# Two banks of a layer-1 attention unit computed on VectorE from thirds of score tiles, and zeros written by transfers

## The chip, the core and the metric

The kernel runs on one core of a Trainium2 chip. The core has five engines with instruction streams of their own: TensorE (PE, with its weight loads PEld) for matmuls, VectorE (DVE), ScalarE (ACT, which computes exponentials), GpSimd (POOL) and SyncE (SP, which here only issues transfers). The metric is the device time of one execution, in microseconds; lower is better. Times of several runs are given with their median.

## The reference

Four attention layers stand one after the other over 2048 positions of width 640, with 32 heads of 20 values. Layers 0 and 2 look back over a window of 256 positions, layers 1 and 3 see all positions. Each adds its output to its input.

```python
def _B_ref(x, wqkv, wo):                      # _A_ref is the same with a mask: 0 <= q - k < 256
    qkv = (x @ wqkv).reshape(B, S, 3, H, Dh).transpose(2, 0, 3, 1, 4)
    q, k, v = qkv[0], qkv[1], qkv[2]
    scores = jnp.einsum("bhqd,bhkd->bhqk", q, k) * (Dh ** -0.5)
    p = _softmax(scores, axis=-1)
    o = jnp.einsum("bhqk,bhkd->bhqd", p, v)
    return o.transpose(0, 2, 1, 3).reshape(B, S, D) @ wo

x = A_x
x = x + _A_ref(_layernorm(x), A_wqkv, A_wo)   # layer 0
x = x + _B_ref(_layernorm(x), B_wqkv, B_wo)   # layer 1
x = x + _A_ref(_layernorm(x), A_wqkv, A_wo)   # layer 2
x = x + _B_ref(_layernorm(x), B_wqkv, B_wo)   # layer 3
```

## The kernel before

The work is cut into units. A unit is a layer, a chunk of 512 queries (c from 0 to 3) and a group of four heads (g from 0 to 7). For each block of 128 keys and each head it has one bank: a matmul of 128 keys by 512 queries that fills one of the eight banks of PSUM. A full unit (layers 1 and 3) has 16 key blocks times four heads, 64 banks; a unit with a window has 12. Layer 1's chunk 0 and layer 3's chunk 0 are done in parts, over ranges of keys (PARTS), since the later keys come into being only while the layer below is finished; their partial sums are kept in a large fp32 tile, part_o["t"] (named raw_o in the profile).

The main loop (the `while` near the end) makes one score tile per turn, a tick. In a tick PE writes the scores of the next three banks (L1186) into PSUM banks 0 to 2 or 3 to 5, in turn; ACT takes the exponential of the whole tile in one instruction (L1206) and writes it to SBUF as the tile pt; and PE multiplies the probabilities of four banks that are two or three ticks old by the values (L1258, "PV"), adding up in PSUM bank 7, called op. When a unit ends, DVE copies op to SBUF (oT, L805), and a tail of small steps on PE and DVE divides by the sums of the rows (L962 to L998). Units with a window have a mask multiplied in on DVE (L1241). Bank 6 serves everything else; it is given out by take_m and drop_m.

Between score tiles a planner places tasks: normalizing (t_ln), projections to q and k (t_block, evacuated by L304 and sent to DRAM from POOL at L507), values (t_v), the output projection (t_out), and tails. Each has a due time, the unit that first needs it, and a cost in PE time; pump() spends a credit per tick on them. The function keep_clock counts PE's activity over the last three ticks and puts in filler matmuls (L612) into bank 6 where there is too little. Weights, and q, k and v of a unit, are fetched by SP (load_unit, L711 to L733), the next unit's ahead of time (load_ahead).

In layer 3's chunks 1 to 3 (but for the first unit) the last key block of each head, four banks of 64, is set aside (Unit.aside). Its scores are written into bank 6 when that is free (L837), and DVE computes the exponential by arithmetic on the bits of the float: t_side yields one DVE instruction after another (L843 to L881, two heads at a time), and side_step takes as many as side["credit"] allows, which grows by SIDE_RATE each tick. side_start takes four tiles of the normalized input, which are free by then, as its work space. At the unit's end PE multiplies the results by the values (L1267).

The strips of 32 partitions that hold a head of 20 values need zeros in their last 12. At the start DVE sets slot 8 of the tile ka_all to zero (L154; PE's warm-up matmuls at L1036 read it too), and a task, t_zeros, lets DVE write zeros to slots 9 to 17 (L1009), the output weights wop (L1013), and the k and q tiles kts and qts (L1018), spread over ticks; then "kas" and "kts" are set as ready, which load_unit's callers ask for (unit_needs). After wop is zeroed, load_wop fetches the output weights into it through SP.

## Time and profile before

| | us |
|---|---|
| median of 5 runs | 2401.8 |
| the five runs | 2407.64, 2408.22, 2400.97, 2401.8, 2400.6 |
| the profiled execution | 2407.64 |
| its span, first to last instruction | 2405.9 |

The profile below is of that one execution. A group's line gives the source line, the engine, what is written and read with its shape, how often, the busy time and the mean duration; after the bar stands the engine's idle time just before these instructions and what ended it. Durations of instructions that follow each other closely overlap, so their sum can exceed the busy time that an engine could spend. A fresh start on one engine often waits for another; the views of waits say for whom. "Granted clock" is the share of its full rate at which TensorE ran.

### The profile page before, as it was taken

The page shows a single profiled execution, that of the slowest core. Times are in us where ns is not written, and L with a number is a line of the kernel's source. Part 1 is how long each engine was busy: PE and PEld are TensorE (multiplying, and loading weights), DVE is VectorE, ACT ScalarE, POOL GpSimd, SP SyncE. Part 2 cuts the span into 40 slices and gives each one's busy share as a digit, 9 for nine tenths or more (in the row PEclk, how much of TensorE's full clock was granted, in tenths as well). Part 3 has the DMA queues.
Part 4 walks back from the last instruction along what each step waited for, and adds up shares of the span by engine and source line. Part 5 has one row for each costly group of instructions (what it writes and reads, how often), then busy time and mean ns, then how long its engine had stood idle before and what let it go on. Part 6 is the DMA issues. An engine that isn't in the chain of part 4 may idle for free.

```text
span 2405.9 us, 40056 instructions
## 1 busy us (share of the span) xinstructions
PE 2024.0 (84%) x15761; PEld 729.1 (30%) x15761; DVE 1273.0 (53%) x2473; ACT 2199.5 (91%) x1738; POOL 136.2 (6%) x284
## 2 busy tenths in 40 slices
PE   7898898888888898888888888888788788888886
PEld 3343333323323342333322333332322121122112
DVE  6676776423323243423352434452667767777776
ACT  6787889899999999999999989999999989999995
POOL 2111110000000001000100001001000000000000
PEclk9798999998999999999998989999855565556556
DMA  3332422322200223102330124022200010111000
GB/s 110 85 94 68 110 69 59 76 62 68 81 19 26 57 71 90 34 13 56 88 91 16 19 74 112 26 41 74 63 29 26 26 37 26 30 34 37 26 13 11
DMA packets 172796, 129.11 MB, mean 54 GB/s; under 512 B 115584, under 2 KB 155904, under 8 KB 172608
## 3 DMA queue, kind: packets, MB, share of 16 engines
q1 hardware_dynamic: 163872, 101.39, 17.0%
q0 software_dynamic: 8736, 25.18, 3.0%
q8 instruction: 123, 2.02, 0.3%
q14 instruction: 65, 0.53, 0.1%
HBM read 98.70 MB, written 27.79 MB: 53 GB/s over the span
## 4 chain that ended last, share of the span: by engine, by line
ACT 37%; PE 31%; issue 16%; DVE 13%; DMA 2%; SPq 1%; POOL 0%; ACTq 0%; DVEq 0%; POOLq 0%
ACT pt L1206 34%; PE ps L1186 8%; PE ps L353 6%; PE ps L1258 5%; PE ps L529 4%; PE ps L612 3%; PE ps L444 3%; ACT ka L1206 2%; DVE pt L1241 2%; DVE st L304 1%; DMA wqk<-in_B_wqkv_dram 1%; DVE on L995 1%; DVE oT L805 1%; DVE xnT L864 1%; DVE x_sb L538 1%
## 5 line engine op out<-in xcount | busy, mean ns | idle before, releaser
L1206 ACT ACTIVATE pt<-ps 128x1536 bf16<-128x1536 f32 (+3 forms) x1586 | 2053.2, 1442 | 144.3 <-PE ps L1186 131.5
L1186 PE MATMUL ps<-qt,kt 32*128 32x512 bf16 x4004 | 641.4, 462 | 231.4 <-ACT pt L1206 174.7
L1258 PE MATMUL ps<-pt,vt 128*21 128x512 bf16 x3744 | 463.6, 453 | 17.6 <-DVE oT L805 15.9
L1186 PEld LDWEIGHTS <-kt 32*128 32x128 bf16 x4004 | 188.6, 94 | 631.6 <-issue 610.7
L1241 DVE TENSOR_TENSOR pt<-pt,masks 128x1024 bf16<-128x1024 bf16 (+5 forms) x403 | 240.8, 625 | 163.8 <-ACT pt L1206 162.7
L353 PE MATMUL ps<-xnT,wqk 128*128 128x512 bf16 x830 | 229.2, 403 | 19.7 <-DMA wqk<-in_B_wqkv_dram 5.5
L612 PE MATMUL ps<-masks,ident 128*128 128x512 bf16 x765 | 230.5, 412 | 7.2 <-DVE st L304 2.7
L1258 PEld LDWEIGHTS <-vt 128*21 128x21 bf16 x4004 | 103.6, 90 | 352.0 <-issue 341.0
L304 DVE CAST st<-ps 128x512 bf16<-128x512 f32 x127 | 87.8, 691 | 196.1 <-PE ps L353 195.3
L529 PE MATMUL ps<-wop,on 128*128 128x320 bf16 x968 | 174.5, 322 | 6.4 <-DVE x_sb L538 3.4
L1186 PE MATMUL ps<-qa,ka 32*128 32x384 bf16 (+2 forms) x1408 | 117.6, 280 | 32.8 <-ACT pt L1206 29.1
L995 DVE TENSOR_TENSOR on<-oT,ps 128x512 bf16<-128x512 bf16 x128 | 87.5, 684 | 107.0 <-PE ps L991 104.2
L538 DVE TENSOR_TENSOR x_sb<-x_sb,ps 128x320 bf16<-128x320 bf16 x120 | 58.1, 484 | 149.5 <-PE ps L529 149.5
L843 DVE TENSOR_SCALAR xnT<-ps 128x512 int32<-128x512 f32 x92 | 63.6, 691 | 128.2 <-PE ps L837 125.1
L1206 ACT ACTIVATE ka<-ps 128x2048 bf16<-128x2048 f32 x65 | 127.1, 1955 | 2.6 <-PE ps L1186 2.2
L444 PE MATMUL ps<-wv,xnT 128*128 128x320 bf16 x640 | 112.4, 309 | 5.7 <-DVE on L995 1.4
L529 PEld LDWEIGHTS <-on 128*128 128x128 bf16 x968 | 90.5, 103 | 76.7 <-issue 41.0
L353 PEld LDWEIGHTS <-wqk 128*128 128x128 bf16 x830 | 72.5, 100 | 121.3 <-issue 55.7
L805 DVE CAST oT<-ps 128x512 bf16<-128x512 f32 x112 | 76.8, 685 | 52.7 <-PE ps L1258 39.0
L612 PEld LDWEIGHTS <-ident 128*128 128x128 bf16 x765 | 67.6, 102 | 112.7 <-issue 74.8
L1258 PE MATMUL ps<-pt,va 128*21 128x384 bf16 (+2 forms) x1408 | 79.6, 292 | 16.8 <-DVE oT L805 12.7
L984 DVE COPY rT<-ps 32x128 bf16<-32x128 bf16 x128 | 26.7, 209 | 92.4 <-PE ps L982 91.9
(91 smaller groups left out, 1438.0 us busy)
## 6 DMA issues: line engine op xcount, KB each, us to landing
vt<-v_d SPq DMA_DIRECT2D x48, 336.0 KB
kt<-k_d SPq DMA_DIRECT2D x192, 80.0 KB
wqk<-in_B_wqkv_dram SPq DMA_DIRECT2D x80, 160.0 KB
wqk<-in_A_wqkv_dram SPq DMA_DIRECT2D x70, 160.0 KB
k_d<-st POOLq DMA_DIRECT2D x75, 128.0 KB, 2.2
q_d<-st POOLq DMA_DIRECT2D x75, 128.0 KB, 2.1
qt<-q_d SPq DMA_DIRECT2D x384, 20.0 KB
v_d<-vs POOLq DMA_DIRECT2D x16, 336.0 KB, 3.1
```

The costliest lines, as they stand in the source:

```text
L304: nc.vector.tensor_copy(out=out_, in_=in_)
L353: nc.tensor.matmul(pq, lhsT=wt[:, dc, :], rhs=xt[:, dc, :], start=(dc == 0), stop=(dc == KD - 1),)
L444: nc.tensor.matmul(pv, lhsT=xt[:, dc, i * P : (i + 1) * P], rhs=wv_sb[l % 2][:, dc, h * HD : (h + 1) * HD], start=(dc == 0), stop=(dc == K ...
L529: nc.tensor.matmul(yp, lhsT=on[:, g, qb * P : (qb + 1) * P], rhs=wop[:, g, i * HD : (i + 1) * HD], start=(last or g == 0), stop=(g == G - 1),)
L538: nc.vector.tensor_tensor(out=xv, in0=had, in1=yp, op=ALU.add)
L612: nc.tensor.matmul(ps[:, b, :], lhsT=ident[:], rhs=masks[:, 0, :], start=True, stop=True)
L805: nc.vector.tensor_copy(out=oT[:], in_=op)
L995: nc.vector.tensor_tensor(out=on[:, g, :], in0=oT[:], in1=zb, op=ALU.mult)
L1186: nc.tensor.matmul(sp[:, i, col * P : (col + qn) * P], lhsT=u.k(kc, j), rhs=u.q(j, q0, qn), start=True, stop=True,)
L1206: nc.scalar.activation(out=pt[:, i:k, b0 * P :], in_=sp[:, i:k, b0 * P :], func=ACT.Exp, scale=SCALE,)
L1241: nc.vector.tensor_tensor(out=pt_[:, i:k, b0 * P :], in0=pt_[:, i:k, b0 * P :], in1=mv_, op=ALU.mult,)
L1258: nc.tensor.matmul(op[32 * j : 32 * j + VW, q0 * P : (q0 + qn) * P], lhsT=u.v(kc, j), rhs=pt[:, i, col * P : (col + qn) * P], start=(first ...
```

## The change

It has two parts. First, slots 8 to 17 of ka_all are set to zero by one instruction at the start, and the zeros of wop, kts and qts are copied from them by transfers that POOL issues; t_zeros starts at its fifth tick instead of its thirteenth and has 11 transfers, one or two a tick, in place of 12 DVE memsets. "kas" is no longer asked for.

Second, in layer 1's chunks 1 to 3 two heads (2 and 3) have their last key block set aside: two banks of a unit's 64. Their scores are not written to bank 6 but as the third bank of a score tile whose other two banks go to ACT: when a tile of the unit is put together, the first time at its start and again three tiles later, two ordinary banks are taken and one that is set aside is added (`extra`). In that tick DVE reads the third bank (side["psum"]) into its work space, and ACT's exponential covers two banks, 1024 columns. The work space is part_o["t"], free between chunk 0's parts of layer 1 and those of layer 3 (side_early). The rest of t_side is the same code with a credit of 0.65 a tick. The last key block's ordinary group has then two banks for PV, and the results that DVE made are multiplied in at the unit's end, as in layer 3. Layer 3 sets aside what it did before, now written as `aside = (0, 1, 2, 3)`.

```diff
-    nc.vector.memset(ka_all[:, G : G + 1, :], 0.0)
+    nc.vector.memset(ka_all[:, G:KA, :], 0.0)
...
-                self.aside = l == 3 and c > 0 and (c, g) != (1, 0)
+
+                if c > 0 and (l, c, g) != (3, 1, 0):
+                    self.aside = (2, 3) if l == 1 else (0, 1, 2, 3)
                 k0, k1 = key_blocks(l, part)
-                kcs = range(k0, k1 - self.aside)
-                sets = [(None, 0, [(kc, 0, 4, 0)], j) for kc in kcs for j in range(4)]
+                sets = [
+                    (None, 0, [(kc, 0, 4, 0)], j) for kc in range(k0, k1) for j in range(4)
+                    if kc < NT - 1 or j not in self.aside
+                ]
...
-            return ["kas"] + [(n, l, c, b) for b in blocks for n in "qk"]
+            return [(n, l, c, b) for b in blocks for n in "qk"]
...
+    def side_early():
+
+        b = part_o["t"]
+        side["tiles"] = [b[:, 2 * n : 2 * n + 2, :].rearrange("p a b -> p (a b)") for n in range(3)]
+        side["tiles"].append(b[:, 6, :].bitcast(BF16))
+        side["out"] = deque([b[:, 7, :].bitcast(BF16).rearrange("p (a b) -> p a b", a=2)])
         side["gen"] = t_side()
+        side_step(False)
...
-                    mseq[0] += 1
-                    mfree[6] = (state["tick"] + 2, mseq[0])
-                    nc.tensor.matmul(
-                        ps[:, 6, :], lhsT=u.k(NT - 1, 2 * pair + i), rhs=u.q(2 * pair + i, 0, 4),
-                        start=True, stop=True,
-                    )
+                    xi, xm, xw, xe = side["tiles"]
+                    if u.l == 3:
+                        mseq[0] += 1
+                        mfree[6] = (state["tick"] + 2, mseq[0])
+                        nc.tensor.matmul(
+                            ps[:, 6, :], lhsT=u.k(NT - 1, u.aside[2 * pair + i]),
+                            rhs=u.q(u.aside[2 * pair + i], 0, 4), start=True, stop=True,
+                        )
+                        side["psum"] = ps[:, 6, :]
...
-                        out=xi.bitcast(I32)[:, i * C : (i + 1) * C], in0=ps[:, 6, :],
+                        out=xi.bitcast(I32)[:, i * C : (i + 1) * C], in0=side["psum"],
...
     def t_zeros():
-        yield ("wait", 12)
-        nc.vector.memset(ka_all[:, G + 1 : KA, :], 0.0)
-        ready.add("kas")
-        yield ("wait", 3)
+        z = ka_all[:, G : G + 4, :].rearrange("p a b -> p (a b)")
+        yield ("wait", 4)
         for n in range(2):
-            nc.vector.memset(wop[:, 4 * n : 4 * n + 4, :], 0.0)
-            yield ("wait", 3)
+            nc.gpsimd.dma_start(
+                out=wop[:, 4 * n : 4 * n + 3, :].rearrange("p g f -> p (g f)"), in_=z[:, 0 : 3 * D]
+            )
+            nc.gpsimd.dma_start(out=wop[:, 4 * n + 3, :], in_=z[:, 0:D])
+            yield ("wait", 1)
         load_wop(0)
         for t in (*kts, *qts):
-            for n in range(0, t.shape[1], S // 2):
-                nc.vector.memset(t[:, n : min(n + S // 2, t.shape[1])], 0.0)
-                yield ("wait", 3)
+            nc.gpsimd.dma_start(out=t[:], in_=z[:, 0 : t.shape[1]])
+            yield ("wait", 1)
         ready.add("kts")
...
+            u = banks[n][0]
+            at = placed.setdefault(id(u), [])
+            extra = []
+            if u.aside and len(at) < 2 and banks[n + 1][0] is u and len(tiles) >= 3 * len(at) + (at or [0])[0]:
+
+                extra = [(u, u.aside[len(at)], "side", 0, [(NT - 1, 0, 4, 0)], False, False, False)]
+                at.append(len(tiles))
+                size = 2
...
-            tiles.append(banks[n : n + size])
+            tiles.append(banks[n : n + size] + extra)
...
+                if cur[-1][2] == "side":
+                    cur = cur[:-1]
+                    n_b -= 1
+                    if side["gen"] is None:
+                        side_early()
+                    while side["at"] != "bank":
+                        side["credit"] = 0.1
+                        assert side_step(False)
+                    side["credit"] = max(side["credit"], 0.1)
+                    side["psum"] = sp[:, n_b, :]
+                    side_step(True)
...
-                side["credit"] = min(side["credit"] + SIDE_RATE, 1.2)
+                side["credit"] = min(side["credit"] + (SIDE_RATE if side["late"] else 0.65), 1.2)
...
-            if len(pts) >= 4 and pts[3][0] <= t - (3 if pts[0][3][0].windowed else 2):
-                group = [pts.popleft() for _ in range(4)]
+            u = pts[0][3][0] if pts else None
+            size = 4
+            if u is not None and u.aside and pts[0][3][4][0][0] == NT - 1:
+                size -= len(u.aside)
+            if len(pts) >= size and pts[size - 1][0] <= t - (3 if u.windowed else 2):
+                group = [pts.popleft() for _ in range(size)]
...
-                    for j in range(4):
+                    for n, j in enumerate(u.aside):
                         nc.tensor.matmul(
                             op[32 * j : 32 * j + VW, :], lhsT=u.v(NT - 1, j),
-                            rhs=pair[j // 2][:, j % 2, :], start=False, stop=True,
+                            rhs=pair[n // 2][:, n % 2, :], start=False, stop=True,
                         )
```

## The prediction

> **What bounds the kernel now.** I read the page's totals, then windows over stages, the groups by shape, the waits, the chain of waits and stretches of the timeline. The totals name the engine that is nearly always at work:
>
> ```profile
> PE 2024.0 (84%) x15761; PEld 729.1 (30%) x15761; DVE 1273.0 (53%) x2473; ACT 2199.5 (91%) x1738; POOL 136.2 (6%) x284
> ```
>
> ACT's exponentials fill 91% of the span, but stages differ. The windows over three stretches (columns: window and its length, busy time and count of PE, PE weight loads, DVE, ACT, POOL; then granted clock, DMA share, GB/s):
>
> ```profile
> 37.00:64.00 27.00, 17.46 (x146) 7.26 (x145) 25.26 (x64) 17.46 (x28) 1.47 (x2) 0.84 0.08 19
> ...
> 483.00:1391.00 908.00, 767.75 (x6316) 293.17 (x6315) 327.43 (x746) 864.05 (x660) 44.59 (x90) 0.94 0.21 53
> ...
> 1710.00:2370.00 660.00, 539.00 (x3407) 144.94 (x3407) 483.56 (x704) 635.08 (x449) 0.00 (x0) 0.55 0.10 28
> ```
>
> From 37 to 64 us, where the zeros are written, DVE is busy 25.26 of 27 us: DVE sets the pace. From 483 to 1391, nearly the whole of layer 1's chunks 1 to 3 (the last sum of chunk 0's parts starts at 501.1, the first partial sum of layer 3 is copied at 1440.6), ACT is busy 95% and DVE 36%. From 1710 to 2370, where layer 3 already has banks on DVE, DVE is busy 73% and ACT 96%. The third window is my yardstick for a DVE under such load. The waits of 483 to 1391 (total us, times, longest) say how ACT loses its other 5%:
>
> ```profile
> PE ps L1186 <- ACT pt L1206: 97.8, 212, 1.0
> ...
> ACT pt L1206 <- PE ps L1186: 39.2, 53, 2.1
> ```
>
> PE waits for ACT 97.8 us; ACT waits for PE 39.2 us (43 with all else). Those 39.2 us lie where PE is slow:
>
> ```profile
> 1028.22 2.32 PE L612 MATMUL ps<-masks,ident 128*128 128x512 bf16 x5
> ...
> 1031.65 18.91 ACT L1206 ACTIVATE pt<-ps 128x1536 bf16<-128x1536 f32 x14 [1.24 <-PE ps L1186]
> ...
> 1033.48 1.25 PE L612 MATMUL ps<-masks,ident 128*128 128x512 bf16 x5
> ```
>
> In the timeline five filler matmuls take 2.32 us at 1028, and 1.25 us at 1033; ACT starved 1.24 us at the slow ones. The middle line also gives ACT's pace when nothing starves it: 14 tiles in 18.91 us, 1.35 us a tile.
>
> **What the Trainium skill says.** (1) ScalarE: Activation LUTs, section "What ACT_TABLE_LOAD costs", gives an ACTIVATE with immediate scale 186 ns + 0.833 ns a column, with about 93 ns of overlap back to back. The trace agrees: 1.35 us between starts against 1.37 by that rule; and 2048-column tiles follow at 1.78 us (1819.17 to 1820.93 and the like), so a bank of 512 costs 0.43 us. (2) VectorE: DVE Perf Modes, section "The perf-mode tier table": tensor_tensor on fp32 stays at 1x, tensor_scalar on fp32 in SBUF gets 2x. The rows agree: 1221 ns against 694 ns for 1024 columns. (3) TensorE: Matmul & The Clock Gate, section "What's actually happening": the array runs at half rate after an idle window of about 3.4 us. The two filler rows above are that factor of nearly two. (4) SBUF — State Buffer, section "SBUF: two separate sides": DVE and GpSimd share a port pair that is held for a whole instruction, so DMAs issued from POOL can wait for DVE. No view here shows POOL blocked.
>
> **Part A, the zeros.** Removed: 12 DVE memsets. The chain of waits (start, length) holds four of them:
>
> ```profile
> 48.74 1.98 DVE ka L1009
> ...
> 55.66 1.12 DVE wop L1013
> ...
> 61.88 1.12 DVE wop L1013
> ...
> 99.57 0.48 DVE kt L1018
> ```
>
> The first three, 4.22 us, lie in the stretch where DVE is 94% busy. Without them DVE still has 21.0 us of work against 17.5 on PE and on ACT, so DVE stays the pace and all 4.2 us go. The kt memset adds 0.48. The other eight (70 to 130 us) lie beside PE and ACT: nothing. So -4.7.
>
> Added: the first memset grows from 256 to 2560 words. By the rows (272 ns for 256, 1978 ns for 2304: 0.833 ns a word) it takes 2.19 us, from 0.93 to 3.12. DVE's next work waits for a load until 4.39: hidden. PE's first warm-up matmul (reads this tile) starts at 2.75 now, so 0.4 us later, with the transposes behind the warm-up. +0.4; below that 0, as the later transposes wait for ACT anyway; above it +2 if the longer memset holds up POOL's mask work.
>
> Added: 11 transfers issued by POOL, four for wop, three kt, four qt, with the row of k_d's issue (551 ns): 6 us between about 25 and 37 us. POOL's L321 memsets of weight tiles stand among them, and DVE's L323 copies wait for those; POOL idles 1.2 to 2.0 us before each memset there, and at most two issues stand between two memsets. +0.4; bounds 0 and +3 (six memsets, 0.5 us each). On SP the four wop loads, with the wait for their zeros, now stand ahead of four wqk loads that were issued at 34.06; their first matmul is at 64.75, so some 30 us hide it: 0. The k and q loads into the zeroed strips come after 74: 0. The windowed loads no longer ask for "kas", but they wait for q and k of their chunk later than that: 0. **A = -4.7 + 0.4 + 0.4 = -3.9.**
>
> **Part B, two banks of each unit.** 24 units (chunks 1 to 3, eight each) give two banks to DVE: 48 score tiles have ACT take 1024 columns where it took 1536. The tile count stays, since the third bank rides in the tile.
>
> ```profile
> L1206 ACT ACTIVATE pt<-ps 128x1536 bf16<-128x1536 f32 x1360 | 1872.8, 1529 | 121.9 <-PE ps L1186 111.7 <-issue 6.2 <-ACT pt L1206 0.9
> ...
> L1206 ACT ACTIVATE pt<-ps 128x1024 bf16<-128x1024 f32 x145 | 149.6, 1033 | 18.8 <-PE ps L1186 16.8 <-DVE st L304 0.4 <-ACT pt L1206 0.2
> ...
> L843 DVE TENSOR_SCALAR xnT<-ps 128x512 int32<-128x512 f32 x92 | 63.6, 691 | 128.2 <-PE ps L837 125.1 <-ACT pt L1206 2.8
> ...
> L864 DVE TENSOR_TENSOR xnT<-xnT 128x1024 f32<-128x1024 f32 x46 | 56.2, 1221 | 0.7
> ...
> L848 DVE TENSOR_SCALAR xnT<-xnT 128x1024 int32<-128x1024 int32 x46 | 31.9, 694 | 1.6
> ```
>
> The means differ by 496 ns, but means contain overlap; I take the pace, 0.43 us: 48 x 0.43 = 20.6 us less ACT work. ACT is at work 95% of the stage; where PE is late the saving is worth nothing: -19.6.
>
> DVE gains, for each unit, by the rows of layer 3's same steps: 2 x 0.691 + 0.694 + 0.694 + 0.693 + 0.686 + 1.221 + 0.691 + 1.219 + 0.684 + 1.222 + 0.689 = 9.9 us; 24 units, 237 us. DVE goes from 327 to about 564 of some 890 us, 63%, below the yardstick's 73%.
>
> Who can wait for it? First, PE: the tile two later may write the third bank only after DVE has read it. The read is ready when the tile's scores are, about one ACT tile (1.35) before ACT begins this tile, and PE needs the bank after ACT's short 0.92: 2.2 us, less the scores' start-up of 0.4. The read takes 0.69, and a mask multiply (0.95 at most) may stand ahead: it fits, with little to spare. Second, the evacuations (st, x_sb, vs, oT, and the tail's small steps) behind a chain step of up to 1.22 us. A step follows the evacuation of its own tick, so it delays the next by 1.22 + 0.69 - 1.35 = 0.6 us at most, and PE uses that PSUM bank again about a tick later. In the yardstick PE's longest item of this kind is oT, 10.2 us in 660, and ACT idles 24 us of 660 (3.7%), less than here (4.8%). But layer 1 has projections and outputs in these ticks and layer 3 hardly has. I take +2.5. Bounds: 0 by the yardstick; above, 0.07 us unhidden in each of about 336 ticks that carry steps (24 units, 14 ticks) is +24.
>
> PE's work falls by 15 fillers and is otherwise equal (48 PV matmuls change their source). In a short tick PE has scores 0.33, PV 0.33 and fewer fillers against ACT's 0.92; a task of five matmuls (1.2) makes it late by half a microsecond, which the next ticks' idle (0.3 to 0.6 in two) takes up. +1.5; bounds 0 and +8 (0.17 in each short tick). The side results are multiplied in at the unit's end, some eight ticks after the last step: no wait. Layer 3's stage keeps its instructions: 0. **B = -19.6 + 2.5 + 1.5 = -15.6.**
>
> **Sum.** -3.9 - 15.6 = -19.5 us. The profiled execution took 2407.6 (span 2405.9, 1.7 around it), so it would take 2388. Of the five runs two stand at 2407.6 and 2408.2, three between 2400.6 and 2401.8; from the median, 2401.8 - 19.5 = 2382.
>
> **Rivals.**
> - PE takes over (chance 0.18). ACT's relief is half lost as the ticks that get shorter are those at a unit's start, where PE also ends the previous unit, and as the half-rate windows (23 windows of 10 us between 480 and 1420 show a mean clock of 0.83 or less) cost the same as before. For: PE is busy 85%. Against: it waits 97.8 us for ACT. B = -6, time 2392.
> - More than I count (0.10). The zeros' stretch leaves PE cold behind it (clock 0.64 from 64 to 80, five projections' matmuls at 2.29 us instead of 1.19); with DVE quicker PE stays warm, 2 to 4 us more, and B has no cost for DVE: 2375.
> - Slower (0.09). DVE becomes the pace: it holds the score tile's third bank and the one spare PSUM bank, PE stops for each, and PE's gaps close its clock, each time costing ACT 1.2 us as at 1031. It decides once more than 0.07 us of each of the 336 ticks is unhidden, or with some 20 more slow windows. For: projections and chain steps fall into the same ticks. Against: the third window. Time about 2412.
> - That the change does not do what it says I exclude: the built order has 48 tiles of 1024 more and 48 of 1536 fewer on ACT.
>
> **How the numbers follow.** Forecast 0.63, with a range of its own from 2374 to 2391 (A from -5.5 to -1, B from -20 to -10); rivals as above. That two runs of five stood 7 us above the median adds to the upper end. The range 2370 to 2396 leaves out the slower rival, the far end of "more", and part of the first rival. About 0.2% (5 us) is what a measurement can tell from no change: faster 0.86 (forecast, "more", most of the first rival), same 0.05, slower 0.09.
>
> **What would show it.** A right: no memset in the chain from 37 to 64, and layer 1's first tile some 4 us sooner. B right: 1312 tiles of 1536 and 193 of 1024; the stage from the last sum of chunk 0 to layer 3's first partial sum shorter by about 16 us, ACT still busy some 94%, DVE about 63%. B wrong: PE waiting for DVE over 30 us in that stage, ACT's idle for PE up from 39 towards 60, or more slices below clock 0.9. The forecast is wrong altogether if layer 3's stage, whose instructions are equal, moves by more than 3 us.

## The result, and the profile after

The changed kernel is slower: its median over 29 runs is 2415.45 us (2404.16 to 2436.77), beside 2406.07 us (2394.85 to 2416.97) for 50 runs of the kernel before. The ratio is 1.0049, with a 95% interval from 1.0035 to 1.0064. The forecast was 2382.

The totals of the page of the kernel after:

```profile
PE 2033.9 (84%) x15746; PEld 726.6 (30%) x15746; DVE 1480.7 (61%) x2748; ACT 2184.0 (91%) x1738; POOL 143.0 (6%) x295
```

ACT has 15.5 us less to do than before and DVE 207.7 us more, as meant. The groups by shape say that the tiles are the ones that were counted, 1312 and 193:

```profile
L1240 ACT ACTIVATE pt<-ps 128x1536 bf16<-128x1536 f32 x1312 | 1815.7, 1505 | 138.2 <-PE ps L1209 128.2 <-issue 4.8 <-ACT pt L1240 1.6
L1240 ACT ACTIVATE pt<-ps 128x1024 bf16<-128x1024 f32 x193 | 200.8, 1041 | 28.3 <-PE ps L1209 24.3 <-PE ps L1005 1.6 <-DVE st L304 0.4
```

So the relief is there, and the time is not. The stage to look at runs from the last sum of chunk 0's parts to the first partial sum of layer 3: chunks 1 to 3 of layer 1. (The forecast put its start at 501.1 us; that is the first of eight such sums. The last is at 554.0 before and at 546.2 after.) Windows over this stage, before (window and length, then busy time and count of PE, PE's loads, DVE, ACT, POOL; clock, DMA share, GB/s):

```profile
554.00:1440.60 886.60, 752.63 (x6173) 288.33 (x6172) 322.24 (x728) 840.29 (x642) 45.63 (x91) 0.93 0.21 53
```

and after, with the last stretch, layer 3's chunks:

```profile
546.20:1443.70 897.50, 761.09 (x6159) 286.58 (x6158) 535.03 (x1015) 825.42 (x642) 47.00 (x91) 0.92 0.21 52
...
1712.80:2412.80 700.00, 564.96 (x3545) 154.73 (x3544) 506.09 (x743) 647.95 (x459) 0.00 (x0) 0.55 0.10 28
```

Read a window's length as ACT's busy time plus ACT's idle time. Before, 886.6 is 840.3 + 46.3. After, 897.5 is 825.4 + 72.1. ACT lost 14.9 us of work and gained 25.8 us of idling. The last stretch kept its length (699.9 before). The waits of the kernel after in the stage (total us, times, longest) say whom ACT and PE wait for:

```profile
PE ps L1209 <- ACT pt L1240: 74.0, 150, 1.0
PE ps L981 <- DVE on L1009: 9.8, 14, 1.4
PE ps L1296 <- DVE oT L809: 9.3, 14, 1.3
PE ps L408 <- DVE xn L399: 5.2, 7, 2.2
...
ACT pt L1240 <- PE ps L1209: 65.3, 95, 2.5
```

The same waits before, from 554.0 to 1440.6 (L967 there is L981 here):

```profile
PE ps L967 <- DVE on L995: 2.5, 5, 0.6
PE ps L408 <- DVE xn L399: 1.7, 5, 0.6
...
ACT pt L1206 <- PE ps L1186: 41.1, 58, 1.9
```

Two of these waits are new in size. L981 is the first matmul of a unit's tail; it waited for DVE 2.5 us in 5 places before. L408, the transposes of the normalized input, waited 1.7 us. All of PE's waits for DVE together rose from 28.4 us (68 times) to 50.0 (99 times), those in the tail from 6.0 to 19.0; and ACT waits for PE's scores 65.3 us where it was 41.1. No wait of PE's scores (L1209) for DVE's read of the third bank is among them. The timeline shows how one can lead to the other, in three places of the kernel after (start, duration, instruction; in brackets the idle time before it and what ended it):

```profile
763.44 0.69 DVE L857 TENSOR_SCALAR raw_o<-ps 128x512 int32<-128x512 f32 x1 [0.42 <-PE ps L1209]
764.05 0.68 DVE L1009 TENSOR_TENSOR on<-oT,ps 128x512 bf16<-128x512 bf16 x1
...
764.78 0.24 PE L981 MATMUL ps<-sel,oT 128*128 128x4 bf16 x4 [1.36 <-DVE on L1009]
...
765.54 2.32 PE L612 MATMUL ps<-masks,ident 128*128 128x512 bf16 x5
...
768.77 1.02 ACT L1240 ACTIVATE pt<-ps 128x1024 bf16<-128x1024 f32 x1 [1.66 <-PE ps L1209]
...
1094.62 0.25 PE L981 MATMUL ps<-sel,oT 128*128 128x4 bf16 x4
...
1094.91 0.69 DVE L862 TENSOR_SCALAR raw_o<-raw_o 128x1024 int32<-128x1024 int32 x1
...
1095.64 0.69 DVE L867 TENSOR_SCALAR raw_o<-raw_o 128x1024 int32<-128x1024 int32 x1
1096.25 0.25 DVE L986 RECIPROCAL rz<-ps 128x16 f32<-128x16 f32 x1
...
1096.55 0.30 PE L529 MATMUL ps<-wop,on 128*128 128x320 bf16 x1 [0.94 <-DVE rz L986]
...
1162.72 1.22 DVE L882 TENSOR_TENSOR raw_o<-raw_o 128x1024 f32<-128x1024 f32 x1
...
1163.86 0.48 DVE L304 COPY xnT<-ps 128x640 bf16<-128x640 bf16 x1
1164.26 0.44 DVE L399 TENSOR_SCALAR xn<-x_sb,rstd,nmr 128x640 bf16<-128x640 bf16 x1
1164.75 0.66 PE L408 MATMUL ps<-ident,xn 128*128 128x128 bf16 x5 [1.13 <-DVE xn L399]
...
1166.59 1.45 ACT L1240 ACTIVATE pt<-ps 128x1536 bf16<-128x1536 f32 x1 [1.33 <-PE ps L1209]
```

At 763 DVE reads the third bank (L857) before it ends a tail's `on` (L1009). `on` holds the spare bank 6, the next tail's L981 needs that bank, and PE stands for 1.36 us, with the scores of later tiles behind L981 in its order. Five fillers then take 2.32 us, nearly twice the 1.25 us that five took elsewhere, and ACT has starved 1.66 us when it starts again at 768.77. At 1094 two chain steps (L862, L867) stand ahead of a tail's rz: its matmuls are done at 1094.87, DVE comes to it at 1096.25, and PE stands 0.94 us for the bank. At 1162 it is a chain step (L882, 1.22 us) that stands ahead of the copy of xnT and the next xn: PE stops 1.13 us at L408, and ACT starves 1.33 us soon after.

### The profile page after: what moved, and what is told of

It is laid out like the page before. It is cut to its first block, busy times and chain, and to the rows that moved or that the text cites. A ratio compares the mean times of both kernels' runs of the same rounds, so it can differ in the third digit from the quotient of the medians.

```text
span 2412.8 us, 40353 instructions
## 1 busy us (share of the span) xinstructions
PE 2033.9 (84%) x15746; PEld 726.6 (30%) x15746; DVE 1480.7 (61%) x2748; ACT 2184.0 (91%) x1738; POOL 143.0 (6%) x295
## 4 chain that ended last, share of the span: by engine, by line
PE 33%; ACT 32%; DVE 17%; issue 16%; DMA 1%; SPq 1%; POOL 0%; ACTq 0%; DVEq 0%; POOLq 0%
ACT pt L1240 29%; PE ps L1209 8%; PE ps L353 6%; PE ps L1296 5%; PE ps L529 5%; PE ps L612 3%; PE ps L444 3%; DVE pt L1275 3%; ACT ka L1240 2%; DVE on L1009 1%; DVE oT L809 1%; DVE st L304 1%; DVE x_sb L538 1%; DMA wqk<-in_B_wqkv_dram 1%; DVE raw_o L857 1%
## 5 line engine op out<-in xcount | busy, mean ns | idle before, releaser
L1209 PE MATMUL ps<-qt,kt 32*128 32x512 bf16 x4004 | 654.3, 466 | 210.1 <-ACT pt L1240 157.2
L1209 PEld LDWEIGHTS <-kt 32*128 32x128 bf16 x4004 | 184.0, 94 | 619.0 <-issue 601.7
L353 PE MATMUL ps<-xnT,wqk 128*128 128x512 bf16 x830 | 228.5, 401 | 20.8 <-DMA wqk<-in_B_wqkv_dram 6.2
L304 DVE CAST st<-ps 128x512 bf16<-128x512 f32 x127 | 87.8, 691 | 174.6 <-PE ps L353 173.7
L529 PE MATMUL ps<-wop,on 128*128 128x320 bf16 x968 | 171.1, 318 | 9.8 <-DVE x_sb L538 4.0
L1209 PE MATMUL ps<-qa,ka 32*128 32x384 bf16 (+2 forms) x1408 | 117.7, 279 | 30.3 <-ACT pt L1240 26.5
L857 DVE TENSOR_SCALAR xnT<-ps 128x512 int32<-128x512 f32 x92 | 63.5, 691 | 128.4 <-PE ps L850 124.3
L1009 DVE TENSOR_TENSOR on<-oT,ps 128x512 bf16<-128x512 bf16 x128 | 87.3, 682 | 60.3 <-PE ps L1005 53.9
L529 PEld LDWEIGHTS <-on 128*128 128x128 bf16 x968 | 90.1, 102 | 77.0 <-issue 42.3
L353 PEld LDWEIGHTS <-wqk 128*128 128x128 bf16 x830 | 72.6, 100 | 123.7 <-issue 57.4
L444 PEld LDWEIGHTS <-xnT 128*128 128x128 bf16 x640 | 56.6, 100 | 48.9 <-issue 29.6
```

Of the source, the lines that this page charges most:

```text
L304: nc.vector.tensor_copy(out=out_, in_=in_)
L353: nc.tensor.matmul(pq, lhsT=wt[:, dc, :], rhs=xt[:, dc, :], start=(dc == 0), stop=(dc == KD - 1),)
L444: nc.tensor.matmul(pv, lhsT=xt[:, dc, i * P : (i + 1) * P], rhs=wv_sb[l % 2][:, dc, h * HD : (h + 1) * HD], start=(dc == 0), stop=(dc == K ...
L529: nc.tensor.matmul(yp, lhsT=on[:, g, qb * P : (qb + 1) * P], rhs=wop[:, g, i * HD : (i + 1) * HD], start=(last or g == 0), stop=(g == G - 1),)
L857: V.tensor_scalar(out=xi.bitcast(I32)[:, i * C : (i + 1) * C], in0=side["psum"], scalar1=SCALE * LOG2E * E23, scalar2=127.0 * E23, op0=ALU ...
L1009: nc.vector.tensor_tensor(out=on[:, g, :], in0=oT[:], in1=zb, op=ALU.mult)
```

## The experiments

All ratios are to the kernel before on the same chip. "Idle" below is ACT's idle time in the stage, "DVE waits" PE's waits for DVE there, "half rate" the time of the stage with the clock at half; each is from one trace, and the executions that were traced lie up to 6.5 us from their kernels' medians. What the rows stand for is told below; the kernels that are not in the table are in the text.

| kernel | ratio (95%) | stage | ACT busy | idle | DVE waits | half rate |
|---|---|---|---|---|---|---|
| before | 1 | 886.6 | 840.3 | 46.3 | 28.4 | 116.0 |
| after | 1.0049 (1.0035 to 1.0064) | 897.5 | 825.4 | 72.1 | 50.0 | 136.5 |
| zeros alone | 0.9984 (0.9968 to 1.0) | 888.9 | 840.3 | 48.6 | 29.0 | 116.0 |
| banks alone | 1.0087 (1.0059 to 1.0115) | 910.1 | 826.1 | 84.0 | 47.9 | 180.9 |
| no polynomial | 0.9939 (0.992 to 0.9958) | 876.7 | 821.4 | 55.3 | 31.4 | 109.2 |
| no third bank | 0.9919 (0.9897 to 0.9942) | 864.2 | 819.6 | 44.6 | 24.4 | 95.6 |
| thirds and steps later | 0.9988 (0.9971 to 1.0004) | 885.1 | 824.2 | 60.9 | 47.3 | 112.6 |
| steps alone later | 1.0042 (1.0021 to 1.0063) | 892.4 | 824.8 | 67.6 | 47.5 | 126.3 |
| steps in gaps | 0.997 (0.9953 to 0.9987) | 880.2 | 821.9 | 58.3 | 39.8 | 95.6 |
| in gaps, and later | 0.9936 (0.9912 to 0.996) | 875.1 | 822.6 | 52.5 | 40.4 | 105.8 |

**Each part alone.** The first is the kernel before with the zeros by transfers (its edit is the change's own first part), the second the changed kernel with the zeros by memsets as before.

```diff
-    nc.vector.memset(ka_all[:, G : G + 1, :], 0.0)
+    nc.vector.memset(ka_all[:, G:KA, :], 0.0)
...
```

```diff
-    nc.vector.memset(ka_all[:, G:KA, :], 0.0)
+    nc.vector.memset(ka_all[:, G : G + 1, :], 0.0)
...
```

> Part A alone: the zeros by transfers, no bank of layer 1 on VectorE. In the changed kernel's trace layer 1's chunk 1 begins 7.8 us sooner than before, so if that gain is the zeros' and stays, this is 5 to 8 us faster than before (ratio 0.997 to 0.998). If the gain is lost again later, or the clock eats it, the ratio is 1.000.

> Part B alone: two banks of a unit on VectorE, the zeros by memsets as before. If the two parts add up and the whole change costs 12 us, this costs 17 to 20 us (ratio 1.007 to 1.008). If the loss comes of the two together, the ratio is nearer 1.002.

Medians 2401.65 and 2425.3. Alone, the zeros gain 0.16%, 3.9 us, with an interval from 0 to 7.7; next to the banks they are worth 0.38% (1.0087 less 1.0049). The loss is all in the second part.

**The steps taken away.** The two reads and the short tiles stay, and one coarse step stands for the ten that turn a pair of banks into exponentials.

```diff
+                if u.l == 1:
+                    while not side["out"]:
+                        yield None
+                    pt = side["out"].popleft()
+                    po = pt.rearrange("p a b -> p (a b)")
+                    V.tensor_scalar(out=po, in0=xi, scalar1=0.0, scalar2=None, op0=ALU.max)
+                    side_out.setdefault(id(u), []).append(pt)
+                    yield 0.7
+                    continue
```

> The changed kernel with the exponential's correction left out in layer 1: DVE does the two reads of the score tile and one step instead of ten, 2.1 us a unit instead of 9.9, so layer 1's two heads have a coarse exponential for their last key block. The 48 short tiles, the order on TensorE and the fillers stay. Theory DVE (its steps hold up the evacuations that TensorE waits for): the loss goes and ScalarE's relief comes, 15 to 25 us faster than before (ratio 0.990 to 0.994). Theory TensorE (short ticks are too short for it, and fewer fillers let its clock fall): still 5 us or more slower than before (1.002 to 1.005).

The median is 2387.42. The window of its stage:

```profile
546.40:1423.10 876.70, 750.52 (x6159) 284.55 (x6158) 365.77 (x799) 821.36 (x642) 45.68 (x91) 0.94 0.21 53
```

The nine further steps of a unit (169 us of DVE's busy time, 535.0 less 365.8) carry the loss: 1.0049 - 0.9939 is 1.1%, 26 us, with some 6 us either way by the two intervals.

**The banks left out.** ACT is relieved and nobody does the two banks: no scores, no reads, no steps, no product with the values.

```diff
+                if cur[-1][2] == "side":
+                    cur = cur[:-1]
+                    n_b -= 1
...
-                    side["psum"] = sp[:, n_b, :]
-                    side_step(True)
```

> The changed kernel with the two banks of each layer-1 unit left out altogether: no scores, no VectorE work, no values product for the last key block of heads 2 and 3. The 48 short tiles on ScalarE stay where they are, with nothing in them for VectorE. If the short ticks themselves are too short for TensorE (which also ends the unit before there): ScalarE's idle time in the first six ticks of the units stays up (13 us before, 27 without the polynomial), and this is no better than without the polynomial, 0.992 to 0.995. If the reads by VectorE make that idle time: it goes back to 13 us and the full 20 us of relief show, 0.988 to 0.990.

The median is 2383.21. Against the zeros alone this is -0.65%, 15.6 us (about 9 to 22 by the intervals): the relief is real. It is not ACT's alone, since PE too loses the 96 matmuls of these banks (scores and values), which the change keeps. Against the run with reads and one step it is -0.2%, which the intervals don't tell from nothing: reading the third bank in its tile is cheap.

**Length and load of the steps.** One kernel cuts every step into two halves of 512 columns and credits them alike; another, with thirds and steps later, computes the middle of the chain in bf16, which trims DVE's load by about a fifth.

```diff
+                for h in range(2) if u.l == 1 else ():
+                    s = slice(h * C, (h + 1) * C)
...
```

```diff
+                    mh, wh = xm.bitcast(BF16)[:, 0 : 2 * C], xw.bitcast(BF16)[:, 0 : 2 * C]
...
```

> The changed kernel with each step on VectorE cut in two of 512 columns, at half the credit each: somewhat more VectorE time in all (20 instructions' overhead in place of 10), but no step over 0.7 us. If the length of a single step is what holds up an evacuation (1.22 us for the products): faster than the changed kernel by 5 us or more (1.001 or lower). If it is VectorE's load as such: as the changed kernel or slower (1.004 to 1.008).

> A version meant to beat both: the thirds nine and twelve tiles after a unit's start, and in layer 1 the steps after the bit operations on 16-bit values, some 7.8 us of VectorE a unit instead of 9.9, no step over 0.7 us. Theory DVE: between the later thirds alone (0.9988) and no polynomial (0.9939), say 0.995 to 0.998. If only the place of the steps matters: 0.9988.

Halves: 1.0058 (1.0038 to 1.0077), median 2417.12. Trimmed: 0.9986 (0.9972 to 0.9999), against 0.9988 untrimmed in the same place. The halves were to bring 5 us or more if length is what costs, the trimmed chain 0.995 to 0.998; neither came. So neither a step's length nor a fifth of the load decides.

**Where reads and steps stand.** First both go nine tiles past the unit's first; then the reads stay and only the steps wait until ten ticks after the first read. In both the credit is 1.05 a tick, which in the order as built puts two steps into one tick in 48 ticks (24 in the change).

```diff
-            if u.aside and len(at) < 2 and banks[n + 1][0] is u and len(tiles) >= 3 * len(at) + (at or [0])[0]:
+            if u.aside and len(at) < 2 and banks[n + 1][0] is u and len(tiles) >= 3 * len(at) + (at or [starts.get(id(u), len(tiles)) + 9])[0]:
```

```diff
+                while u.l == 1 and state["tick"] < side["from"] + 10:
+                    yield None
```

> The changed kernel with the two thirds placed nine and twelve tiles after a unit's start instead of at its start and three tiles on, so that VectorE's steps begin when the tail of the unit before is through; the credit for the steps is 1.05 a tick so that they end in time. Theory DVE, in the form that the steps collide with the tail: faster than before by 8 us or more (0.993 to 0.997). Theory DVE in the form that any task's evacuation is held up: about the changed kernel's 1.003 to 1.005. Theory TensorE: as the changed kernel, 1.003 to 1.006.

> The changed kernel with the reads of the score tile where they are (a unit's start and three tiles on), and the ten steps on VectorE held back until ten ticks after the first read, at a credit of 1.05 a tick. It parts the steps' place from the reads' place. If the steps collide with the tail of the unit before: as with both moved, 0.997 to 1.000. If it is the reads that collide: as the changed kernel, 1.003 to 1.006.

Medians 2402.02 and 2412.99. Moving both gives 0.6% back; moving the steps alone gives nothing that can be told. The sums of DVE waits hardly differ from after's (47.3 and 47.5, against 50.0). Summed by the code that waits, the tail's share falls from 19.0 to 5.6 and 11.7 us, and that of the transposes (L408) and the output projection (L529) rises from 11.5 together to 19.0 and 17.2: steps put elsewhere by a fixed number of ticks meet other evacuations of the same bank. These sums are as large in the kernel that gains as in the one that doesn't, so they alone don't say what a place costs.

**Fillers and the tail's own pace.** Does the clock alone carry the loss? keep_clock counts two banks in a short tile though PE does three. One kernel counts three (764 fillers instead of 750); one adds to this a demand 15% higher, for 882 fillers; one lets the tail wait three ticks instead of two between its steps (864 fillers, as the planner's order shifts); and one counts three with thirds and steps later.

```diff
-                state["heat"] += 0.414 * n_b
-                work.append((state["heat"], 1.0 * n_b))
+                state["heat"] += 0.414 * (n_b + third)
+                work.append((state["heat"], 1.0 * (n_b + third)))
```

```diff
+                more = 1.15 if u.l and u.c and side["gen"] is not None else 1.0
...
+                work.append((state["heat"], more * (n_b + third)))
```

```diff
+        late = side["gen"] is not None and not side["late"]
-        yield ("wait", 2)
+        yield ("wait", 2 + late)
...
```

> The changed kernel with keep_clock counting a short tick as three banks, which TensorE computes in it, so that 14 fillers come back. If too few fillers let TensorE's clock fall: less half-rate time in layer 1 than the changed kernel's 136 us and 5 us or more faster than it (1.002 or lower). If the stalls for VectorE are the cause: as the changed kernel or slower by the fillers' time (1.004 to 1.007).

> As the run that counts three banks, with keep_clock's aim raised by 15% from layer 1's chunk 1 on: 882 fillers in place of 764. If the falling clock turns short stops into lost time: mean clock up from 0.827, and faster than that run's 1.0017 by 3 us or more. If the stops themselves are the loss: the fillers' TensorE time is added, 1.003 or more.

> The changed kernel with one tick more before each of a tail's three steps on TensorE from layer 1's chunk 1 on (864 fillers come out of the planning). If TensorE's stops at the tail (19 us in layer 1's trace against 6 before) carry the loss: those waits fall to 6 us or so and time falls to 1.000 or lower, below the run with more fillers. If not: as the run with more fillers.

> The thirds nine and twelve tiles after a unit's start, and keep_clock counting a short tick as three banks; arithmetic as in the changed kernel. If the two gains add: 0.9988 - 0.003 = 0.996. If the later place had already mended what the fillers mend: 0.998 to 0.999.

Counting three: 1.0017 (1.0002 to 1.0033), median 2409.65, with 126.3 us of its stage at half rate. This is what was expected if too few fillers let the clock fall: 14 fillers give back 0.3% of the change's loss, some 8 us (3 to 13). More fillers: 1.006 (1.0041 to 1.0078), median 2419.77, although its profiled execution had a clock of 0.832 and 112.6 us at half rate, less than the kernel before. So a part of the loss goes with the clock; but the better clock that 118 more fillers bring comes with more time, not less. That was expected if PE's stops are the loss and the fillers' own time on PE is added; no run measures that time apart. The slower tail: 0.999 (0.9976 to 1.0004), median 2404.09; but its trace doesn't show why. PE's waits at the tail were 20.0 us, not fewer, its stage was 895.8, and of the 11 us by which its trace is shorter than after's 6 lie in layer 3's chunks, whose instructions it leaves as they are. It is left unexplained. Count three with both later: 0.9994 (0.998 to 1.0008), median 2405.31, no more than the later place alone: there the 14 fillers bring nothing.

**The relief taken back.** ACT covers the third bank too, with everything else as in the change, so that only the relief should go.

```diff
+                    w = k + third
-                        out=pt[:, i:k, b0 * P :], in_=sp[:, i:k, b0 * P :],
+                        out=pt[:, i:w, b0 * P :], in_=sp[:, i:w, b0 * P :],
```

> The changed kernel with ScalarE still taking three banks in the 48 ticks (the third's result is not used), so that VectorE's steps are added and nothing is taken from ScalarE. If the steps cost TensorE some 27 us, as the run without the polynomial says: 20 to 28 us slower than before (1.008 to 1.012). If the steps cost only where ticks are short: about before with the zeros' gain, 0.998 to 1.002.

It gave 1.0173 (1.0147 to 1.0198), median 2445.61, which can't be read as a price of the relief, since a new wait came in. ACT's waits in its stage:

```profile
ACT pt L1242 <- PE ps L1209: 46.5, 70, 1.8
ACT pt L1242 <- DVE raw_o L857: 30.1, 35, 2.6
```

ACT now waits 30.1 us for DVE's read of the same bank. The Trainium skill, "PSUM — Partial Sum Buffer", section "PSUM bank collisions raise a hardware error", says that two engines must not be in one bank and quadrant at once, two readers included, and that the back end orders them; this trace fits that. The run is inconclusive for the question it was made for.

**One step a bank.** The read itself yields a coarser exponential as a 16-bit integer that is the bits of a bf16: no chain at all. Once at the unit's start, once twelve and fifteen tiles later with three banks counted. In the first the earliest result lands in a plane of part_o whose partial sum of chunk 0's last group is still to be read, so that sum is changed.

```diff
+                        V.tensor_scalar(
+                            out=po.bitcast(I16), in0=side["psum"],
+                            scalar1=SCALE * LOG2E * 128.0, scalar2=127.0 * 128.0 - 7.4,
+                            op0=ALU.mult, op1=ALU.add,
+                        )
```

> The changed kernel with one VectorE instruction for each bank in layer 1: it multiplies and adds straight from the score tile into a 16-bit integer that is the bfloat16 of a piecewise linear exponential (a coarser exponential for two banks of a unit's 64). 1.4 us of VectorE a unit. Theory DVE load: as without the polynomial or a little better, 0.990 to 0.995. If the reads at the unit's start are what costs: 0.998 or more.

> As the run with one step, with the thirds at twelve and fifteen tiles after the unit's start, where the kernel before has almost no half-rate time and ScalarE idles least, and with keep_clock counting a short tick as three banks. If the short ticks cost because TensorE has no room for them at a unit's start: faster than the one-step run by 5 us or more, 0.987 to 0.991. If the place does not matter without the polynomial: equal to the one-step run.

0.9961 (0.9944 to 0.9978), median 2394.01, and 0.9941 (0.9921 to 0.9962), median 2387.12. Without the chain the second part pays in either place; the intervals don't part the two places, and neither came to what was hoped for it. The second run takes both its places for quiet ones, and only one is: summed over the 24 units, ACT of the kernel before idles 4.3 to 5.5 us at each of the tiles 11 to 13 after a unit's start, and at most 1.9 us at each from 14 on; its half-rate time ends there too.

**Steps rather where the spare bank is free.** So far the length of a step, a fifth of the load and a fixed delay of the steps alone had brought nothing; the guess that was left is that a step stands in DVE's order ahead of an evacuation for which PE waits. The gate below issues a step only in a tick in which no task has used bank 6, one step a tick; nine ticks after the last read (three in the second kernel) it opens. The second kernel also puts the thirds six tiles later.

```diff
-                side["credit"] = min(side["credit"] + (SIDE_RATE if side["late"] else 0.65), 1.2)
-                side_step(False)
+                if side["late"]:
+                    side["credit"] = min(side["credit"] + SIDE_RATE, 1.2)
+                    side_step(False)
+                elif mfree[6][0] <= state["tick"] or state["tick"] >= side.get("read", 0) + 9:
+                    side["credit"] = min(side["credit"] + 1.05, 0.7)
+                    side_step(False)
```

> The reads stay where the change puts them (ticks 0 and 3 of a unit). A step is only issued in a tick in which no task has used the spare bank (from nine ticks after the last read on, in any tick), one step a tick. In the instruction order, steps that stand right ahead of one of the tail's small DVE operations on the spare bank (rz, rT, on) fall from 84 to 37; steps ahead of other evacuations do not fall. If the loss comes from steps that stand ahead of the tail's operations in DVE's queue: PE's waits for DVE at the tail fall from 19 us to about 12, as without any steps, and the ratio to before falls from 1.0049 to 0.998 or lower. If the number of stops only moves to other evacuations (as when all steps were put ten ticks later, 1.0042), PE's waits for DVE stay at 45 to 50 us and the ratio stays at 1.003 to 1.006.

> The same gate (released three ticks after the last read), with the two thirds six and nine tiles after the unit's first instead of at its start. Reads and steps then both keep clear of the tail before. If keeping clear of the tail is all that matters, this is at least as good as both nine tiles later without the gate (0.9988): 0.996 to 0.999, with PE's waits for DVE at the tail near 6 us. If DVE's load costs wherever it is put, 0.999 to 1.003 and PE's waits for DVE stay near 47 us in sum.

Steps in gaps: 0.997, median 2395.03, with the same ten steps a unit as the change. Windows of its stage:

```profile
546.20:1426.40 880.20, 736.03 (x6089) 283.27 (x6158) 539.58 (x1015) 821.92 (x642) 47.16 (x91) 0.95 0.21 53
```

and its waits there:

```profile
PE ps L1209 <- ACT pt L1241: 82.9, 169, 1.0
...
PE ps L981 <- DVE on L1009: 7.2, 10, 1.4
PE ps L408 <- DVE xn L399: 5.2, 14, 0.6
...
ACT pt L1241 <- PE ps L1209: 50.2, 67, 2.6
```

(PE's count is lower since 69 of its matmul records are missing in this trace; its weight loads are all there.) DVE is as busy as in the change (539.6 against 535.0 us), and yet ACT waits for PE's scores 50.2 us where the change had 65.3, and the longest wait of the transposes is 0.6 us, not 2.2. The tail's waits are 11.1 us in sum, close to the 12 expected and to the 11.6 of the kernel without the chain. So it is the order, not the load: this edit alone moves the ratio by 0.79%, some 19 us (14 to 24) of the 26. With the later place it comes to 0.9936, median 2387.93, better than the 0.996 to 0.999 that was expected:

```profile
544.90:1420.00 875.10, 737.41 (x6086) 281.78 (x6155) 540.79 (x1016) 822.56 (x642) 49.44 (x91) 0.94 0.22 53
```

This version keeps the arithmetic of the change and beats both kernels, by 0.64% and about 1.1%. It stands where the kernel with one coarse step stood (0.9939), though with its reads elsewhere: what the steps still cost is no longer told from nothing, within some 7 us. Its waits for DVE at the tail are 7.4 us, all of them 40.4.

The gate does less by itself than its name says. In the order as built only 60 of the first kernel's 240 steps are issued under its condition, 180 after it has opened, and in the second kernel 18 and 222; so for the most part it puts the steps later, and one to a tick. Even so they stand in other ticks. Steps that share a tick with a task's use of bank 6 (its evacuation is issued in that tick):

| kernel | steps of 240 | ratio |
|---|---|---|
| after | 158 | 1.0049 |
| steps alone later | 115 | 1.0042 |
| thirds and steps later | 95 | 0.9988 |
| in gaps, and later | 85 | 0.9936 |
| steps in gaps | 73 | 0.997 |

The two go together but for the last pair. That the bank is the reason is supported by this and by the waits, not proved: the two kernels with the gate also never have two steps in a tick, and no run has that pace without the gate.

## Why the prediction was wrong

**Right: the zeros, to the digit by luck.** -3.9 was predicted, and the zeros alone gave 0.9984, 3.9 us of 2406, with an interval from 0 to 7.7. (Thirteen memsets go, not twelve; the one left out was among those priced at nothing.) The sign that was named is there: layer 1's first score matmul starts at 173.0 before, at 168.2 with the zeros alone and between 166.9 and 168.7 in all other kernels with transfers but one (173.7). With memsets and banks it starts at 170.9, so about 2 us of this are scatter. The stage's start is a weaker witness: over all the traces it scatters from 544.9 to 556.1.

**Right, as far as it was tested: ACT's relief.** The forecast had -19.6 and +1.5 for PE in the short ticks, -18.1 in sum. With the two banks left out the runs gave -15.6 (9 to 22), PE's relief of 96 matmuls included, and in the stage ACT's busy time fell by 20.7 us, as 48 x 0.43 says, with no more idling than before (44.6 us against 46.3). The tile counts and DVE's share (60% against 63%) came as predicted, and layer 3's stage did not move.

**Right: the read of the third bank.** The forecast found that it fits "with little to spare". Its price with one further step is 0.2%, not told from nothing. It does join in at 763 above, where it stands ahead of a tail.

**Wrong: the +2.5 us for the evacuations behind a chain step.** This term of the sum failed: nine steps of ten cost 26 us (21 to 32), ten times as much, and about the upper bound of 24 that stood beside it. Two parts of its working gave way. The first: "A step follows the evacuation of its own tick, so it delays the next by 1.22 + 0.69 - 1.35 = 0.6 us at most." In the order of the changed kernel the 240 steps form 167 groups, of which 53 are two to four steps in a row, and reads, multiplications by masks and oT fall in the same ticks. So DVE came 1.4 us late for the tail at 1096. Rows by themselves are not the harm: with the gate 47 of 132 groups have two to nine steps, and that kernel is faster. The lateness can be measured. The stage has 331 evacuations of the spare bank; from the end of their matmuls to their start they wait 26.7 us in sum before and 67.0 us after. More than 0.6 us late are 6 of them before and 43 after, and with the gate 24, with 41.3 us in sum. That "PE uses that PSUM bank again about a tick later" is true and makes it worse: in the three places shown the next task on bank 6, or the next input from DVE, is wanted just then, and PE stands for it with all scores behind. The second: the yardstick. Layer 3's chunks have DVE at 73%, and PE's largest wait for it is 10.2 us in sum, but they lack most of the work that shares the spare bank: from 1710 to 2370 there is no matmul of a projection to q and k and no transpose of the input, while 483 to 1391 has 272 matmuls of the former (L353). The text of the forecast named this difference and then took +2.5 all the same. The share of busy time was the wrong measure; what counted was where the steps stood. The gate shows it: equal load, other ticks, 19 us less. That what matters about a tick is the use of the one bank fits the waits and the counts above.

**The rival that came true.** "DVE becomes the pace: it holds the score tile's third bank and the one spare PSUM bank, PE stops for each, and PE's gaps close its clock" had a chance of 0.09 and a time of 2412; the median is 2415. Its point of decision, 0.07 us unhidden in each of 336 ticks, was met: 26 us are 0.08. What it named for a wrong B came too: PE waiting for DVE over 30 us (50.0), ACT's idle for PE towards 60 (65.3). But DVE was not the pace, at 60% of the stage, and of the two banks that the rival names the waits show the spare one, not the third. It came true in its number and in part of its mechanism.

**What stays open.** How the loss divides between PE's stops and the half-rate windows that follow them: over the traces idle time goes with both, and fillers give back 0.3% where they are few and lose it where they are many. How the gain of the kernels with the gate divides between other ticks, a freer bank and no two steps in a tick. Why the later place, whose waits for DVE sum up to as much as after's, still gains 0.6%: neither the sum of waits nor the lateness of the evacuations (46.1 us with the steps alone later, 46.8 with the thirds too, 47.8 with the gate and the later place) puts those three kernels in their order. And what the slower tail changes, which is level with the kernel before at 53.2 us of waits.

## What to carry to other kernels

Work given to an idle engine costs little by its sum and much by its place: ask what stands behind each new instruction on that engine, which buffer that holds, and whether the engine that wants the buffer next stops for it with other work behind. An engine at 36% with one spare buffer between it and the pacemaker can have little slack in the ticks that use the buffer, and plenty in the others; with 73 of 240 steps in such ticks instead of 158 a loss of 0.5% became a gain of 0.3%, and with the reads moved too, one of 0.6%. A yardstick stage must share the traffic on that buffer, not just the engine's load.

## What the runs showed of the hardware

**Time goes with the granted clock.** Over 184 runs of the kernel before, in five sets, the time rises by 1.4 to 1.6 us for each 0.001 that the mean granted clock of a run falls; the kernel after has the same slope, 1.5. Mean clocks were 0.8297 before and 0.8233 after. At this slope that is 9.6 us, as much as the medians differ; yet the kernel with more fillers has 0.8317 and is slower still, so the clock is not a cause to be taken alone. It does tell how to read a single trace: the stretch between the stage and layer 3's chunks took from 263.0 us (12.4 us at half rate) to 272.8 us (47.6 at half rate) in kernels whose instructions there were the same or nearly so. A difference of a few microseconds in one trace is no evidence.

**Half rate without an idle window.** PE was busy 83 to 86% of the stage and still ran at half rate for 88.7 to 211.6 us of it, by kernel. The Trainium skill, "TensorE: Matmul & The Clock Gate", section "A second HAM failure mode: psum-queue depth-cycling", tells of a kernel in which short idling between groups of matmuls makes the clock go down and up again. Here no stop of PE in the stage of the kernel after, whatever it waited for, was longer than 2.2 us, less than the 3.41 us that the shortest stretch of one rate lasts in its records. So the idle window of some 3.4 us, of which the forecast's third point speaks, is not in this stage, and the half rate is.
